# GpSimd's row sends behind marks of their point, the spectrum's negation a step sooner, and batch 0's rows stored by halves

## The chip, the cores and the metric

One core of one Trainium2 chip runs the whole program. The metric is the device time of one execution in microseconds (us). Three runs of the kernel before gave 1586.66 to 1594.67 us, median 1590.22.

## What is computed

For 8 batches of 2496 x 256 numbers: a Fourier transform along the sequence, a complex 256 x 256 mix of each frequency with a soft threshold, and the inverse transform. The 19968 rows of the result then go through a mixture of 8 experts, of which each row takes the best one.

```python
X = np.fft.rfft(x, axis=1)
Xr, Xi = (X.real.astype(np.float32), X.imag.astype(np.float32))
Yr = Xr @ w_r - Xi @ w_i + b_r
Yi = Xr @ w_i + Xi @ w_r + b_i
Yr = np.sign(Yr) * np.maximum(np.abs(Yr) - lam, 0.0)     # Yi alike
y = np.fft.irfft(Yr + 1j * Yi, n=x.shape[1], axis=1)
...
logits = x @ w_gate + modality_bias[modality_id]         # x: rows of y
e_idx = np.argmax(logits, axis=1)
...
h = np.maximum(x[mask] @ w1[e], 0.0)
out[mask] = gate_w[mask, None] * (h @ w2[e])
```

## The kernel before

The transform over 2496 = 39 x 64 points is done in matrix products. **Stage 1** (`s1_split`, `s1_chunk`) transforms over 39 points, in 11 chunks a batch: each chunk is split into a high and a low part (on GpSimd, L251, for chunks 0 to 5 of batches 2 and up), three products are summed, ScalarE copies them into a buffer `ev` (L275), and every two chunks SP stores the buffer to a scratch in DRAM, `scr` (L279). There are three such buffers. For batch 0 this is the program's start.

**The pairs**, ten points p a batch: `a_load` reads two of the 20 frequencies back from the scratch (L287), `s2_pair` transforms them (L296) and splits the result into `Xh` (ScalarE, L301, and the negated copy of the imaginary part, L303) and `Xl` (VectorE, L302 and L304); `mix_sums` has 24 products with the mixing matrix (L333); `shrink` is the soft threshold, on ScalarE (L341, `u`) and VectorE (L342, `s`); `is2_pair` transforms back over 64 (L357) into a buffer `z`. The loop is skewed: at point i it does the load of i+4, `s2` of i+2, the mix of i+1 and the inverse of i.

**The inverse over 39**, 22 pivots j a batch: `pivot` turns three columns of `z` with two products (L373, four instructions in a row) and splits them on ScalarE (L378, `ph`) and VectorE (L379, `pl`); `is1`, two pivots behind, has three products (L385 to L387) and a copy (L388). The stage 1 chunks 2 to 10 of batch b+2 stand between the pivots of b, so batches 6 and 7 have none.

**The route** of a batch (`Route.route`) runs beside the pairs of the next one: it finds each row's expert and its place, and at the end puts 22 sends on a list, `pending`. A send (`Route.scatter`, L541) is an indirect DMA from GpSimd that writes 117 rows of 264 numbers to their places in DRAM. GpSimd also splits the experts' weights (`SplitWeights.step`, L982 and L983), whose stores (L984, L985) SP issues. Four engines (TensorE, ScalarE, VectorE, GpSimd) run in the order in which the program is written; SP's loads and stores are held in place by `issue_after`. The sends are called at points 6 to 9, four at each, and one more ahead of each pivot, until the list is empty:

```python
                    if p > 5:
                        rt.scatter(4)
...
                for j in range(J):
                    rt.scatter(1)
                    pend.append((j, at.pivot(b, j)))
```

A send waits for its rows and its places alone, and for the landing of the eighth send before it.

**The experts** follow in 78 tiles of 256 rows: SP loads rows (L769) and weights (L751), two products per expert layer (L808, L838), and GpSimd sends the results (L851). The rows of the last batch are sent while the first tiles run.

## Time and profile before

| | |
|---|---|
| median of three runs | 1590.22 us |
| the profiled execution's own time | 1600.25 us |
| its span, first to last instruction | 1598.5 us |
| mean granted TensorE clock (share of full speed) | 0.975 |
| busy: TensorE, VectorE, ScalarE, GpSimd | 95%, 43%, 39%, 39% |
| first product of the experts (L808) | 686.37 us after the start |
| sends of rows (L541) before 680 us | 154, of 1.0 us each |

The busy shares are means over the span. The stages differ: the start, up to some 50 us; then one batch per 76 to 79 us, the pairs in 43 and the inverse in 26 to 32; and the experts from 686 us on. A view of a stretch tells more than the mean.

### The profile page before, as it was taken

To read this page: it belongs to the slowest core of one execution; us is meant where nothing else is said; L and a number is where in the kernel's file an instruction comes from. 1 tells how busy PE (TensorE), PEld (TensorE's weight loads), DVE (VectorE), ACT (ScalarE), POOL (GpSimd) and SP (SyncE) were. 2 spreads that over 40 slices of the span, in tenths; PEclk is the share of its full clock that TensorE was granted. 3 is DMA by queue.
4 is the path that set the end of the run, shared out by engine and by line. 5 is a ranking of instruction groups with operands and counts; after the bars stand their busy time and mean duration, and the time that the engine had idled before them with its cause. 6 is when DMAs were issued, how large, how long until landed. Compare 5 with 4: busy or idle time off the path is not lost. (4 is left out here: it accounts for less than half of the span.)

```text
span 1598.5 us, 34701 instructions
## 1 busy us (share of the span) xinstructions
PE 1521.1 (95%) x12459; PEld 1484.9 (93%) x12459; DVE 689.7 (43%) x1435; ACT 625.2 (39%) x1281; POOL 625.1 (39%) x629
## 2 busy tenths in 40 slices
PE   5899999999999889699999999999999999999998
PEld 4799898989898889599999999999999999899998
DVE  4466555656565555254333333333333333233332
ACT  4365656565656344242232323232223223232232
POOL 0054747475657544423642222232223223222232
PEclk8899999999999989799999999999999999999999
DMA  8788686858686536622442522752225227735441
GB/s 275 208 257 265 189 244 206 267 170 263 182 257 193 183 115 223 180 80 50 92 128 53 156 42 53 249 163 44 46 49 158 45 41 262 236 60 163 142 134 44
DMA packets 289103, 246.68 MB, mean 154 GB/s; under 512 B 207168, under 2 KB 242388, under 8 KB 285217
## 3 DMA queue, kind: packets, MB, share of 16 engines
q1 hardware_dynamic: 269937, 202.85, 44.9%
q0 software_dynamic: 18992, 41.58, 7.7%
q8 instruction: 100, 1.64, 0.4%
q14 instruction: 74, 0.61, 0.1%
HBM read 434.30 MB, written 100.73 MB: 335 GB/s over the span
## 5 line engine op out<-in xcount | busy, mean ns | idle before, releaser
L838 PE MATMUL y<-w,hh 128*128 128x256 f32 x2496 | 436.5, 278 | 0.0
L808 PE MATMUL h<-xh,w 128*128 128x256 f32 x2496 | 403.9, 278 | 3.8 <-DMA w<-wsp 3.8
L838 PEld LDWEIGHTS y<-w,hh 128*128 128x128 f32 x2496 | 378.4, 188 | 0.7 <-ACT hh L810 0.2
L838 PE MATMUL y<-w,hl 128*128 128x256 f32 x1248 | 347.6, 279 | 0.5 <-DVE hl L811 0.4
L808 PEld LDWEIGHTS h<-xh,w 128*128 128x128 f32 x2496 | 340.0, 189 | 4.3 <-issue 3.5
L851 POOL DMA_INDIRECT out<-o,ix x161 | 158.8, 986 | 430.5 <-ACT o L830 393.0
L811 DVE SCALAR_TENSOR_TENSOR hl<-h,hh 128x512 fp32r<-128x512 f32 x312 | 209.5, 689 | 231.8 <-ACT hh L810 192.1
L808 PE MATMUL h<-xl,w 128*128 128x256 f32 x1248 | 245.4, 278 | 0.0
L810 ACT ACTIVATE hh<-h 128x512 fp32r<-128x512 f32 x312 | 178.4, 596 | 155.4 <-PE h L808 140.9
L838 PEld LDWEIGHTS y<-w,hl 128*128 128x128 f32 x1248 | 234.2, 188 | 1.7 <-DVE hl L811 1.3
L333 PE MATMUL mx<-wmix,Xh 128*128 128x256 f32 x1280 | 187.3, 289 | 5.5 <-issue 4.7
L808 PEld LDWEIGHTS h<-xl,w 128*128 128x128 f32 x1248 | 189.5, 189 | 0.0
L788 POOL TENSOR_TENSOR xl<-tr,xh 128x512 fp32r<-128x512 f32 x78 | 101.1, 1296 | 206.7 <-ACT xh L787 205.4
L828 DVE TENSOR_SCALAR o<-y,xt 128x256 f32<-128x256 f32 x78 | 37.7, 484 | 316.9 <-ACT o L830 312.6
L333 PEld LDWEIGHTS mx<-wmix,Xh 128*128 128x128 f32 x1280 | 166.8, 194 | 8.2 <-issue 6.7
L830 ACT ACTIVATE o<-y,xt 128x256 f32<-128x256 f32 x78 | 37.1, 475 | 345.5 <-PE y L838 345.5
L373 PE MATMUL pv<-pv,z 128*120 128x136 f32 x704 | 115.8, 291 | 4.6 <-ACT z L360 4.3
L379 DVE TENSOR_TENSOR pl<-pv,ph 120x264 fp32r<-120x264 f32 x176 | 75.4, 431 | 102.0 <-ACT ph L378 73.9
L373 PEld LDWEIGHTS pv<-pv,z 128*120 128x120 f32 x704 | 103.2, 193 | 12.6 <-ACT z L360 5.8
L342 DVE SCALAR_TENSOR_TENSOR s<-mx,u 128x512 f32<-128x512 f32 (+1 forms) x81 | 55.5, 685 | 125.5 <-ACT u L341 113.9
L333 PE MATMUL mx<-wmix,Xl 128*128 128x256 f32 x640 | 103.0, 284 | 1.8 <-issue 1.8
L983 POOL TENSOR_TENSOR wl<-wr,wh 128x512 fp32r<-128x512 f32 x64 | 82.6, 1291 | 49.2 <-DMA wsp<-wl 46.3
(184 smaller groups left out, 2059.2 us busy)
## 6 DMA issues: line engine op xcount, KB each, us to landing
w<-wsp SPq DMA_DIRECT2D x166, 2048.0 KB
a<-scr SPq DMA_DIRECT2D x160, 128.0 KB
xt<-xs SPq DMA_DIRECT2D x624, 32.0 KB
scr<-ev SPq DMA_DIRECT2D x40, 480.0 KB
x<-in_x SPq DMA_DIRECT2D x37, 512.0 KB
wr<-in_moe_w SPq DMA_DIRECT2D x64, 256.0 KB
wsp<-wh SPq DMA_DIRECT2D x64, 256.0 KB
wsp<-wl SPq DMA_DIRECT2D x64, 256.0 KB
```

The costliest lines, as they stand in the source:

```text
L333: self.nc.tensor.matmul(ps[i][:, i, :], t[:, 2 * i + c, o:o + 128], self.w[:, wi, c, lo, :], start=False, stop=n == len(ops) - 1, skip_gro ...
L342: nc.vector.scalar_tensor_tensor(s, ps, LAM, u, ALU.add, ALU.min)
L373: nc.tensor.matmul(ps[:PK, c * 128:c * 128 + D // 2 + E], self.z[:, o:o + 3, :, :].rearrange("p n k r -> p (n k r)"), self.pv[:, c, :], st ...
L379: nc.vector.tensor_sub(pl, ps[:PK, :GC], ph)
L788: nc.gpsimd.tensor_sub(xl, tr, xh)
L808: nc.tensor.matmul(ps[:, q, :], w1[:, lo, c, f * 128:(f + 1) * 128], x[:, c, :], start=n == 0, stop=n == 5)
L810: nc.scalar.activation(hh[:, 2 * p:2 * p + 2, :], ps, AF.Relu)
L811: nc.vector.scalar_tensor_tensor(hl[:, 2 * p:2 * p + 2, :], ps, 0.0, hh[:, 2 * p:2 * p + 2, :], ALU.max, ALU.subtract)
L828: nc.vector.tensor_scalar_mul(o[:, s, :], y[s], gate)
L838: nc.tensor.matmul(y[s], lhsT, w2[:, lo, f, :], start=n == 0, stop=n == 23)
L851: ins = self.nc.gpsimd.indirect_dma_start(out=self.out, out_offset=bass.IndirectOffsetOnAxis(ap=ix, axis=0), in_=o, in_offset=None, bounds ...
L983: nc.gpsimd.tensor_sub(lo, raw, hi)
```

## The change

Three edits. First, `scatter` takes a mark, an instruction for which the sends of that call must wait. At points 6 to 9 one send waits for the negation that `s2` has just issued, and a second one for the `shrink` of the mix: eight sends in the pairs instead of sixteen. The other fourteen stand behind the pivots, one for each step of `j * 14 // 22`, and each waits for the `pl` of its pivot; the last is behind the last pivot. Second, `s2_pair` issues ScalarE's negation ahead of VectorE's first subtraction. Third, batch 0's stores are cut in two: partitions 0 to 59 of each buffer when it is full, the loads of pairs 0 to 3 behind the last of these, and partitions 60 to 119 after the loads. The load of pair 3 and the second step of the mixing matrix (`next(mixing)`) move accordingly.

```diff
--- before.py
+++ after.py
@@ -161,7 +161,7 @@
         self.ps = pool("ps", 2, space=PSUM)
         self.dr = pool("dr", 2, space=DRAM)
         self.scr = [None] * nb
-        self.xt, self.xs = {}, {}
+        self.xt, self.xs, self.parts = {}, {}, []
 
     def consts_first(self):
 
@@ -275,8 +275,19 @@
         nc.scalar.copy(self.ev[:, 2 * h:2 * h + 2, :].rearrange("p j d -> p (j d)"), ps[:PK])
         if h == 1 or c == 10:
             n = min(4, J - 4 * u)
-            rows = self.scr[b].rearrange("k (g j) d -> (k g) j d", g=3)
-            self.stored = nc.sync.dma_start(rows[:, 4 * u:4 * u + n, :], self.ev[:, :n, :])
+            if b == 0:
+                self.parts.append((self.ev, u, n))
+                self.s1_store(self.ev, u, n, 0, 60)
+            else:
+                self.s1_store(self.ev, u, n, 0, PK, b)
+
+    def s1_store(self, ev, u, n, lo, hi, b=0):
+        rows = self.scr[b].rearrange("k (g j) d -> (k g) j d", g=3)
+        self.stored = self.nc.sync.dma_start(rows[lo:hi, 4 * u:4 * u + n, :], ev[lo:hi, :n, :])
+
+    def s1_rest(self, b):
+        for ev, u, n in self.parts:
+            self.s1_store(ev, u, n, 60, PK)
 
 
     def a_load(self, b, p):
@@ -299,8 +310,8 @@
         xh = self.w2.tile([128, 4, 192], F32R, tag="Xh", name=f"Xh_{b}_{p}")
         xl = self.w2.tile([128, 4, 192], F32R, tag="Xl", name=f"Xl_{b}_{p}")
         nc.scalar.copy(xh[:, :, 64:192], ps)
+        self.mark = nc.scalar.mul(xh[:, :, 0:64], ps[:, :, 64:128], -1.0)
         nc.vector.tensor_sub(xl[:, :, 64:192], ps, xh[:, :, 64:192])
-        nc.scalar.mul(xh[:, :, 0:64], ps[:, :, 64:128], -1.0)
         nc.vector.tensor_sub(xl[:, :, 0:64], xh[:, :, 128:192], ps[:, :, 64:128])
         return xh, xl
 
@@ -339,7 +350,7 @@
         u, s = tl(self.w1, "u"), tl(self.w2, "s")
         ps = ps[beg][:, beg:end]
         nc.scalar.activation(u, ps, AF.Relu, bias=self.nlam)
-        nc.vector.scalar_tensor_tensor(s, ps, LAM, u, ALU.add, ALU.min)
+        self.mark = nc.vector.scalar_tensor_tensor(s, ps, LAM, u, ALU.add, ALU.min)
         return s
 
     def is2_pair(self, b, p, parts):
@@ -376,7 +387,7 @@
         ph = self.w2.tile([PK, GC], F32R, tag="ph", name=f"ph_{b}_{j}")
         pl = self.w2.tile([PK, GC], F32R, tag="pl", name=f"pl_{b}_{j}")
         nc.scalar.copy(ph, ps[:PK, :GC])
-        nc.vector.tensor_sub(pl, ps[:PK, :GC], ph)
+        self.mark = nc.vector.tensor_sub(pl, ps[:PK, :GC], ph)
         return ph, pl
 
     def is1(self, b, j, ph, pl, copy):
@@ -536,11 +547,13 @@
         nc.gpsimd.tensor_scalar_add(x1[:, :, 129], self.tok[:, j0:j1], float(b * SEQ))
         self.pending += [(si, j - j0, x1[:, j - j0, :]) for j in range(j0, j1)]
 
-    def scatter(self, n):
+    def scatter(self, n, mark=None):
         for si, k, rows in self.pending[:n]:
             i = self.nc.gpsimd.indirect_dma_start(
                 out=self.xs, out_offset=bass.IndirectOffsetOnAxis(ap=si[:, k:k + 1], axis=0),
                 in_=rows, in_offset=None, bounds_check=E * REG - 1, oob_is_err=False)
+            if mark is not None:
+                self.order(i, mark)
             self.note(i)
         self.pending = self.pending[n:]
 
@@ -1050,14 +1063,18 @@
                 ins = load(0)
             with tc.issue_after(ins.ins):
                 ins = load(1)
-            next(mixing, None)
+            with tc.issue_after(ins.ins):
+                load(2)
+                ins = load(3)
             at.s1_split(1, 0)
             at.s1_split(1, 1)
-            for c in range(4):
-                with tc.issue_after(ins.ins):
+            with tc.issue_after(ins.ins):
+                at.s1_rest(0)
+                for c in range(4):
                     at.s1_chunk(1, c, 2 if c < 2 else 0)
+                    if c == 1:
+                        next(mixing, None)
             with tc.issue_after(ins.ins):
-                load(2)
                 at.table_load("q", 0)
                 ins = at.s1_load(1, 2)
             bias(0)
@@ -1066,9 +1083,6 @@
             s2(1)
             at.s1_split(1, 4)
             mix(0)
-            with tc.issue_after(ins.ins):
-                ins = load(3)
-
             state = None
             routing = iter(())
             for b in range(nb):
@@ -1111,7 +1125,7 @@
                     if p < 6 if b > 0 else p > 4:
                         sw.step()
                     if p > 5:
-                        rt.scatter(4)
+                        rt.scatter(1, at.mark)
                     if p < 9:
                         bias(i + 2)
                     ending = i == last - 2
@@ -1119,6 +1133,8 @@
                         mix_last(i + 1, 0)
                     else:
                         mix(i + 1, 0 if apart else None)
+                    if p > 5:
+                        rt.scatter(1, at.mark)
                     if due:
                         state = next(routing, None)
                     at.is2_pair(b, p, ss.pop(i))
@@ -1143,8 +1159,9 @@
                     at.s1_chunk(*s1.pop(0), 0)
                 pend = []
                 for j in range(J):
-                    rt.scatter(1)
                     pend.append((j, at.pivot(b, j)))
+                    if j * 14 // 22 != (j - 1) * 14 // 22:
+                        rt.scatter(1, at.mark)
                     chunk = j % 2 == 1 and j != 15
                     if len(s1) > 4 and chunk:
                         at.s1_split(*s1[4])
@@ -1158,6 +1175,7 @@
                     next(routing, None)
                 for _ in routing:
                     pass
+                assert not rt.pending
                 bias(10 * b + 11)
                 ahead(10 * b + 10)
                 for jj, r in pend:
```

GpSimd's order in batch 1, from the split of chunk 1 of the batch after next at point 5 to the first pivots (`xs` are the rows in DRAM, `x1b` the results of the inverse, `si` the places, `x1l` the low part of a stage 1 chunk, `wh` a weight split). Before, where rows that repeat are folded into a count:

```order
L251 TENSOR_TENSOR x1l_1_1840<-x_0_1517,x1h_1_1839 117x512
L541 DMA xs<-x1b,si_0_1710 162048x264 x4
L251 TENSOR_TENSOR x1l_2_1906<-x_1_1586,x1h_2_1905 117x512
L541 DMA xs<-x1b,si_0_1710 162048x264 x4
L251 TENSOR_TENSOR x1l_3_1974<-x_1_1586,x1h_3_1973 117x512
L541 DMA xs<-x1b,si_0_1710 162048x264 x4
L251 TENSOR_TENSOR x1l_4_2049<-x_2_1651,x1h_4_2048 117x512
L541 DMA xs<-x1b,si_0_1710 162048x264 x4
L251 TENSOR_TENSOR x1l_5_2115<-x_2_1651,x1h_5_2114 117x512
L541 DMA xs<-x1b,si_0_1710 162048x264 x6
L982 CAST wh_6_2287<-wr_6_1734 128x512
```

And now, with what each waits for:

```order
L251 TENSOR_TENSOR x1l_1_1846<-x_0_1523,x1h_1_1845 117x512 [waits PE_49,Activation_49]
L552 DMA xs<-x1b,si_0_1716 162048x264 [waits DVE_49,Activation_49]
L552 DMA xs<-x1b,si_0_1716 162048x264 [waits DVE_49]
L251 TENSOR_TENSOR x1l_2_1906<-x_1_1592,x1h_2_1905 117x512 [waits PE_49,Activation_49]
L552 DMA xs<-x1b,si_0_1716 162048x264 [waits Activation_49]
L552 DMA xs<-x1b,si_0_1716 162048x264 [waits DVE_49]
L251 TENSOR_TENSOR x1l_4_2037<-x_2_1657,x1h_4_2036 117x512 [waits PE_49,Activation_49]
L552 DMA xs<-x1b,si_0_1716 162048x264 [waits Activation_49]
L552 DMA xs<-x1b,si_0_1716 162048x264 [waits DVE_49]
L251 TENSOR_TENSOR x1l_5_2097<-x_2_1657,x1h_5_2096 117x512 [waits PE_49,Activation_49]
L552 DMA xs<-x1b,si_0_1716 162048x264 [waits DMASW0_49,DVE_49]
L552 DMA xs<-x1b,si_0_1716 162048x264 [waits DMASW1_49,DVE_49]
```

Two sends instead of four stand between two subtractions, each behind ScalarE or VectorE, and the rest follow behind VectorE (the last two rows here are the first two of the fourteen), with a split of weights after six and one after twelve. The waits on DMASW are those for the eighth send before.

ScalarE and VectorE at the first pair (`s_0_0` is the transform in PSUM), before:

```order
L301 CAST Xh_0_308<-s_0_0_303 128x4x128 [waits PE_49]
L303 ACTIVATE Xh_0_308<-s_0_0_303 128x4x64 [waits DVE_49]
L301 CAST Xh_1_319<-s_0_1_314 128x4x128 [waits PE_49]
L302 TENSOR_TENSOR Xl_0_309<-s_0_0_303,Xh_0_308 128x4x128 [waits Activation_49]
L304 TENSOR_TENSOR Xl_0_309<-Xh_0_308,s_0_0_303 128x4x64 [waits Activation_49]
```

Now:

```order
L312 CAST Xh_0_317<-s_0_0_312 128x4x128 [waits PE_49]
L313 ACTIVATE Xh_0_317<-s_0_0_312 128x4x64
L312 CAST Xh_1_328<-s_0_1_323 128x4x128 [waits PE_49]
L314 TENSOR_TENSOR Xl_0_318<-s_0_0_312,Xh_0_317 128x4x128 [waits PE_49,Activation_49]
L315 TENSOR_TENSOR Xl_0_318<-Xh_0_317,s_0_0_312 128x4x64
```

ScalarE's negation waits for nothing but its place in the queue, and VectorE's second subtraction has lost its wait.

SP's order at the start, from batch 0's last store on (`scr_139` is batch 0's scratch, `scr_261` and `scr_269` batch 1's, `a_n` the load of pair n). Before:

```order
L279 DMA scr_139<-ev_5_236 120x512
L287 DMA a_0_243<-scr_139 64x2x256 x2
L287 DMA a_1_246<-scr_139 64x2x256 x2
L279 DMA scr_261<-ev_0_262 120x1024
L279 DMA scr_261<-ev_1_282 120x1024
L287 DMA a_2_294<-scr_139 64x2x256 x2
L186 DMA c_q<-in_c_q 128x512
L239 DMA x_66<-in_x 128x1024
L287 DMA a_3_357<-scr_139 64x2x256 x2
L186 DMA c_m<-in_c_m 128x512
```

And now, without the load of pair 1, and of the six stores of the second halves the first and the last:

```order
L286 DMA scr_139<-ev_5_236 60x512
L298 DMA a_0_243<-scr_139 64x2x256 x2
L298 DMA a_2_249<-scr_139 64x2x256 x2
L298 DMA a_3_252<-scr_139 64x2x256 x2
L286 DMA scr_139<-ev_0_140 60x1024
L286 DMA scr_139<-ev_5_236 60x512
L186 DMA c_q<-in_c_q 128x512
L286 DMA scr_269<-ev_0_270 120x1024
L186 DMA c_m<-in_c_m 128x512
L286 DMA scr_269<-ev_1_294 120x1024
L298 DMA a_4_368<-scr_139 64x2x256 x2
```

The loads of pairs 2 and 3 stand ahead of batch 1's stores and of the tables, and six more stores stand behind them, ahead of the first table.

## Rows read from the trace of the kernel before

**Rows 1.** The page, part 1: busy time, share of the span and instructions of each engine.

```profile
PE 1521.1 (95%) x12459; PEld 1484.9 (93%) x12459; DVE 689.7 (43%) x1435; ACT 625.2 (39%) x1281; POOL 625.1 (39%) x629
```

**Rows 2.** Busy time by stretch: the stretch and its length, then the busy time of TensorE (PE), its weight loads (PEld), VectorE, ScalarE and GpSimd (POOL) with their instructions, the granted TensorE clock, the DMA share and GB/s. The first five hold the last points of the pairs and the first half of the inverse of batches 1 to 5, the sixth is in the experts.

```profile
160.00:200.00 40.00, 36.38 (x279) 33.76 (x278) 21.17 (x44) 24.12 (x55) 31.69 (x32) 1.00 0.65 190
240.00:280.00 40.00, 37.67 (x284) 35.10 (x284) 22.07 (x48) 24.57 (x59) 31.60 (x32) 1.00 0.68 206
320.00:360.00 40.00, 36.38 (x257) 33.47 (x256) 21.12 (x45) 24.15 (x58) 28.37 (x29) 0.96 0.59 173
400.00:440.00 40.00, 37.39 (x267) 34.81 (x267) 21.37 (x48) 24.55 (x60) 26.49 (x28) 0.96 0.63 183
480.00:520.00 40.00, 37.40 (x284) 34.87 (x283) 21.16 (x48) 25.98 (x62) 28.25 (x32) 1.00 0.65 192
800.00:1000.00 200.00, 200.00 (x1732) 199.13 (x1732) 70.49 (x131) 61.46 (x112) 65.60 (x61) 1.00 0.36 86
```

**Rows 3.** The same view with the inverses of batches 0, 1, 6 and 7 as stretches, from the first product of the first pivot to the last product of the last.

```profile
105.20:131.02 25.82, 25.82 (x192) 24.33 (x191) 16.94 (x38) 19.91 (x50) 13.28 (x13) 1.00 0.86 268
177.81:208.19 30.38, 26.83 (x191) 24.43 (x192) 16.73 (x37) 20.47 (x51) 19.79 (x21) 1.00 0.67 194
571.29:599.81 28.52, 23.30 (x166) 21.91 (x165) 15.03 (x50) 12.73 (x35) 17.12 (x18) 0.88 0.40 134
655.12:686.54 31.42, 24.52 (x156) 23.53 (x157) 10.22 (x24) 14.79 (x44) 11.35 (x12) 0.78 0.41 120
```

**Rows 4.** GpSimd's timeline: start and duration in us, engine, line, operation, output and inputs, count, and in brackets the idle time before it and what ended it. Batch 1's first four sends, then the first and the last of twelve in batch 6's pairs, the first and the eighth in its inverse, the first and last of twelve and of ten in batch 7.

```profile
160.52 1.20 POOL L541 DMA_INDIRECT xs<-x1b,si  x1 [0.21 <-DVE Xl L302]
...
164.62 0.99 POOL L541 DMA_INDIRECT xs<-x1b,si  x1 [0.30 <-issue]
165.64 1.29 POOL L251 TENSOR_TENSOR x1l<-x,x1h 117x512 fp32r<-117x512 f32 x1
...
540.48 1.08 POOL L541 DMA_INDIRECT xs<-x,si  x1 [2.17 <-DVE x L535]
...
554.80 0.99 POOL L541 DMA_INDIRECT xs<-x,si  x1 [0.30 <-issue]
...
570.86 1.02 POOL L541 DMA_INDIRECT xs<-x,si  x1 [0.23 <-issue]
...
579.97 1.00 POOL L541 DMA_INDIRECT xs<-x,si  x1 [0.30 <-issue]
...
628.96 1.09 POOL L541 DMA_INDIRECT xs<-x1b,si  x1 [0.19 <-issue]
...
643.34 0.99 POOL L541 DMA_INDIRECT xs<-x1b,si  x1 [0.31 <-issue]
...
655.42 1.03 POOL L541 DMA_INDIRECT xs<-x1b,si  x1 [0.24 <-issue]
...
667.16 1.00 POOL L541 DMA_INDIRECT xs<-x1b,si  x1 [0.31 <-issue]
```

**Rows 5.** ScalarE's timeline, same columns: the rectifier of the soft threshold around the runs of twelve sends in batches 6 and 7.

```profile
537.37 0.69 ACT L341 ACTIVATE u<-mx,nlam 128x512 f32<-128x512 f32 x1
...
541.98 0.69 ACT L341 ACTIVATE u<-mx,nlam 128x512 f32<-128x512 f32 x1 [0.37 <-issue]
...
555.78 0.69 ACT L341 ACTIVATE u<-mx,nlam 128x512 f32<-128x512 f32 x1 [9.51 <-remote]
...
566.05 0.69 ACT L341 ACTIVATE u<-mx,nlam 128x512 f32<-128x512 f32 x1 [0.68 <-PE mx L333]
...
630.83 0.69 ACT L341 ACTIVATE u<-mx,nlam 128x512 f32<-128x512 f32 x1 [0.57 <-ACT mx L313]
...
646.32 0.69 ACT L341 ACTIVATE u<-mx,nlam 128x512 f32<-128x512 f32 x1 [9.07 <-remote]
```

**Rows 6.** TensorE's timeline, same columns: products of the inverse in batch 6 behind its eight sends, in batch 7 behind its ten, and two pivots, ten apart, after the sends have ended.

```profile
579.44 0.35 PE L385 MATMUL i<-ph,c_g 120*117 120x264 f32 x1 [2.27 <-issue]
...
582.82 0.57 PE L385 MATMUL i<-ph,c_g 120*117 120x264 f32 x1 [2.21 <-ACT x1b L388]
...
667.70 0.57 PE L385 MATMUL i<-ph,c_g 120*117 120x264 f32 x1 [4.97 <-ACT x L388]
...
675.99 0.63 PE L373 MATMUL pv<-pv,z 128*120 128x136 f32 x4
...
684.29 0.63 PE L373 MATMUL pv<-pv,z 128*120 128x136 f32 x4
```

**Rows 7.** SP's queue: start of the issue, duration until the last of the group is issued, line, operation, count. The first loads of pairs from batch 0's scratch, the first weights of the experts, and the weights that follow the last send of batch 6's rows.

```profile
26.73 2.59 SPq L287 DMA_DIRECT2D a<-scr  x4
...
631.02 0.94 SPq L751 DMA_DIRECT2D w<-wsp  x2
...
671.29 27.02 SPq L751 DMA_DIRECT2D w<-wsp  x4
```

**Rows 8.** Groups by line in the first 680 us: line, engine, operation, shape and count, then busy time and mean ns of one, then the idle time of the engine just before them and what ended most of it.

```profile
L303 ACT ACTIVATE Xh<-s 128x256 fp32r<-128x256 f32 x80 | 30.8, 385 | 91.6 <-DVE Xl L302 78.3 <-DVE omid L450 6.3 <-issue 6.3
```

**Rows 9.** TensorE's timeline at the start, columns as in rows 6: the first two pairs' transform, the third pair's, and a stage 1 chunk of batch 1.

```profile
30.37 3.78 PE L296 MATMUL s<-c_m,a 128*128 128x128 f32 x16 [5.57 <-DMA a<-scr]
...
41.95 2.05 PE L296 MATMUL s<-c_m,a 128*128 128x128 f32 x8 [4.83 <-issue]
...
74.88 0.59 PE L270 MATMUL s<-x1h,c_f 117*120 117x512 f32 x1 [2.79 <-DVE x1h L250]
```

## The prediction

> **What bounds the kernel now.** I read the page first: TensorE is busy for 95% of the span [rows 1]. Then the busy time by stage, because an average hides where the other 5% lies. In the expert phase nothing can be won: TensorE is busy for all 200 us between 800 and 1000 [rows 2]. The idle time is in the first 690 us, and in the windows that hold the last points of the pairs and the inverse of each batch. In those of batches 1 to 5 TensorE is idle for 3.62, 2.33, 3.62, 2.61 and 2.60 us of 40 [rows 2]. The inverse of batch 0 has no rows to send and no idle time in its 25.82 us; that of batch 1 takes 30.38 us with 26.83 busy, of batch 6 28.52 with 23.30, of batch 7 31.42 with 24.52 and a granted clock of 0.78 [rows 3]. So I looked at what GpSimd does there.
>
> GpSimd's timeline shows the sends back to back, one per 1.30 us, of which 1.00 is busy. In batch 1 they come by fours, with a subtraction of 1.3 us between the fours (160.52 to 164.62, then L251). In batches 6 and 7, which have no such subtraction, twelve come in one piece: 540.48 to 554.80 and 628.96 to 643.34. Then ten more follow in the inverse: the first eight at 570.86 to 579.97 in batch 6, all ten at 655.42 to 667.16 in batch 7 [rows 4]. Against these, ScalarE's timeline: the rectifier L341 runs every 4.6 us (537.37, 541.98), then not until 555.78, 9.51 us idle, "remote"; and again 9.07 us before 646.32 [rows 5]. Both ends lie 0 to 2 us behind the last send of a run. TensorE has the same in the inverse: 2.27 and 2.21 us idle at 579.44 and 582.82, 4.97 at 667.70 just behind the send of 667.16, while at 675.99 to 684.29, with no send, ten pivots take 8.30 us, 0.83 each [rows 6]. In each piece the first four to six sends cost nothing visible. My reading: while GpSimd issues sends without a gap, instructions and signals of the other engines arrive late; they live off what is already queued, and stop when that is used up.
>
> **The change, part by part.** Durations are of the profiled execution, 1600.25 us, which lies 10 us (0.6%) above the median of the runs, 1590.22. I take the sum off the median, since the terms are stalls of some us that are small against either.
>
> *The runs of twelve in the pairs.* What they cost is the time between rectifiers beyond 4.6 us [rows 5]: 541.98 to 555.78 is 13.8, so 9.2; the next two steps to 566.05 are 10.27 instead of 9.2, so 1.1 of half clock; 630.83 to 646.32 is 15.49, so 10.9. Together 21.2 us. After, points 6 to 9 hold two sends each, one behind ScalarE's negation and one behind VectorE's shrink of its own point: two per 4.6 us with 2.3 us on average from one to the next, less dense than the fours of batch 1, which passed. In the marked sends the wait also regulates itself, since a late engine holds the next send back. Bounds: 0 (the stall isn't the sends') to 21.2. I take **19.5**; the rest is the 2048 KB loads issued at 631.02 [rows 7], which share the stretch with batch 7's run.
>
> *Batches 1 to 5.* The idle times of the five windows add up to 14.8 us [rows 2], and 0.96 of the clock in two of them is 1.6 us each, 18.0 in all. What waits there is mostly the inverse, with ten sends. After, it holds fourteen, one per 1.57 pivots. With chunks of batch b+2 between them a pivot takes 25.82 / 22 = 1.17 us [rows 3], so a send comes every 1.84 us instead of 1.30, and 0.84 us of it is free instead of 0.30. Two splits of the experts' weights stand between GpSimd's sends there; their stores are wanted much later. Bounds: 4 x 5 more sends at today's 18.0 / 50 = 0.36 us, a loss of 7.2, to a gain of 18.0. I take **8**, since four fifths of the sends keep close company still.
>
> *The inverses of 6 and 7.* With 0.83 us a pivot and some 1.7 us to start and end, 20 us would do [rows 6]; batch 7 takes 31.42, and loses 11.4. Batch 6 loses 5.2 of idle time and 2.1 by half clock from 582.82 to 587 (4.2 us at half speed), 7.3. Together 18.7, or 0.94 us a send. Here the pace is 1.57 x 0.83 = 1.30 us a send, just that of a run without gaps, so the marks will hold sends back but leave little free time: fourteen alone need 18.2 us of GpSimd. Bounds: eight more sends at 0.94, a loss of 7.5, to a gain of 18.7. I take **10**, the middle of the part above zero.
>
> *Negation sooner.* It now follows the first copy on ScalarE at once. That engine stood idle for 78.3 us in 80 negations waiting for VectorE's L302, 0.98 us each [rows 8]. The first three products of a half need Xh, so a late Xh would be 0.9 us nearer; but the pairs are bound by TensorE's own sums, and only a pair that comes late uses it. Bounds -1 to +3; I take **0.5**.
>
> *Batch 0's stores by halves.* The first load from the scratch was issued at 26.73; TensorE waited 5.57 us for it until 30.37, then 4.83 us until 41.95, then 2.79 at 74.88 [rows 7, 9]. Now the loads of pairs 0 to 3 follow six stores of half the rows, and should be issued some 4 us sooner. Behind them stand six more stores on SP's queue, and batch 1's first copy into a store buffer waits until the second half has left it, which delays the sums ahead of the first pair by 2 to 3 us. Pair 2 no longer waits for a load. Bounds: a loss of 3 (the first pair late, nothing won behind) to a gain of 7 (5.57 + 4.83 less what the tables still need); I take **3**. The Trainium skill, "DMA: Bandwidth & Descriptors", in its table of patterns, says of two transfers to halves of the partitions not to bother, as they share the same engines and serialize. By it the first half lands at half time only because the other half is queued behind the loads, and the term is between 0 and 3; no run here shows it yet.
>
> *Behind the last batch.* The load at 671.29 is ordered behind the last send [rows 7]. That send moves from the fifth pivot to the last one, and the stage in front of the experts gets some 20 us shorter, while the loads need as long as before. Bounds 0 to 6 us of waiting; I take **-2**.
>
> Sum: 19.5 + 8 + 10 + 0.5 + 3 - 2 = 39 us, so 1590.2 - 39 = **1551 us**.
>
> **The rivals.**
> A, full cure: no stall is left, 21.2 + 18.0 + 18.7 + 3.5 - 2 = 59 us, 1531. For it: the marks regulate themselves, and the first sends of a run are free. Against it: the pace in batches 6 and 7.
> B, the stall is counted by sends in the inverse, at today's mean, (18.0 + 18.7) / 70 = 0.52 us: 98 sends take 51 of the 36.7 that they take now, so 14 of the 19.5 are given back, and 1584 is left.
> C, the other side: in the inverse no send is free, since a pivot is a chain over TensorE, ScalarE and VectorE with two steps in hand, and a send per 1.57 pivots hits each of them. At the 0.94 us of batches 6 and 7 the 98 sends cost 92 us against 36.7; with 21 won elsewhere (19.5 + 3.5 - 2), 34 us slower, 1624. It decides from (36.7 + 21) / 98 = 0.59 us a send. For it: 0.94 was measured. Against it: in these two batches the stall came behind the fourth or fifth send of a piece, and batches 1 to 5 show 0.36.
> D, late transfers: the experts' first rows and weights wait for the sends at the end of batch 7 and the shorter stage, 15 to 20 us of the gain come back as idle time of TensorE around the first tiles: 1570. For it: the order behind the last send. Against it: two loads of weights are issued ahead of it.
> E, it isn't the sends: the stalls coincide with them but come from the loads, and stay; 1590 - 3.5 + 2, some 1588. Against it: batch 6's run has no large load beside it, and stalls as long. The Trainium skill, "SBUF — State Buffer", on its two sides, holds that TensorE, ScalarE and VectorE's own port never wait on anyone and that a transfer and an engine's work can't slow each other; by this alone a gap between sends would bring nothing, which is rival E. The 9.51 us of ScalarE speak against it.
>
> **Chances.** Forecast 0.50 (1538 to 1568), A 0.17, B 0.10, C 0.08, D 0.10, E 0.05. A measurement tells some 0.5%, 8 us, from no change: faster is under 1582, slower over 1598. Faster takes the forecast, A, D and half of B, 0.82; the same is the other half of B and E, 0.10; slower is C, 0.08. The range, 1528 to 1582, takes in A, the forecast's bounds and D, and leaves B's upper half, C and E out, somewhat under 2 in 10.
>
> **What will show it.** Right: no two sends of a piece 1.30 us apart in the pairs; no gap over 2 us before L341's successor in batches 6 and 7; the two inverses at 23 to 26 us; batches 1 to 5 with under 2 us idle in their windows; the first pair's sums near 30 to 34 us and no wait of 4.83 behind them. Wrong: an inverse longer than before (C), gaps in the same places with spaced sends (E), or the first product of the experts waiting for a transfer for over 5 us (D).

## The result, and the profile after

The changed kernel takes 1551.86 us (median of four runs, 1548.6 to 1553.75), the kernel before 1590.93 in the same comparison: a ratio of 0.9753, 95% interval 0.9723 to 0.9783, 39 us faster. The profiled execution took 1551.3 us with a span of 1549.5.

Busy time by stretch, columns as in [rows 2, 3]; the five windows of batches 1 to 5, then the inverses of batches 1, 6 and 7:

```profile
160.00:200.00 40.00, 40.00 (x315) 38.37 (x314) 24.06 (x50) 26.73 (x62) 29.80 (x29) 1.00 0.66 192
240.00:280.00 40.00, 39.90 (x307) 37.93 (x307) 23.81 (x50) 27.98 (x66) 32.48 (x33) 1.00 0.79 232
320.00:360.00 40.00, 39.83 (x307) 37.86 (x306) 25.45 (x54) 26.87 (x66) 28.14 (x29) 1.00 0.76 227
400.00:440.00 40.00, 40.00 (x322) 38.66 (x321) 24.42 (x55) 25.62 (x62) 24.50 (x25) 1.00 0.85 262
480.00:520.00 40.00, 38.68 (x318) 37.38 (x317) 24.25 (x52) 21.35 (x50) 22.04 (x27) 1.00 0.72 220
...
179.02:204.80 25.78, 25.78 (x192) 24.29 (x191) 16.74 (x37) 19.92 (x51) 20.02 (x20) 1.00 0.77 224
542.01:566.94 24.93, 21.41 (x166) 19.97 (x165) 14.89 (x49) 12.84 (x36) 20.20 (x21) 1.00 0.45 145
610.72:637.90 27.18, 20.39 (x155) 18.97 (x156) 10.12 (x24) 14.59 (x44) 16.49 (x18) 0.99 0.65 158
```

Where 2.3 to 3.6 us were idle [rows 2], now at most 0.2 are, in batch 5's window 1.3. The inverse of batch 1, with fourteen sends in it, is as long as that of batch 0 with none. In the inverses of batches 6 and 7 the granted clock is back at 0.99 and above, and 3.5 and 6.8 us of idle time are left.

GpSimd's timeline, columns as in [rows 4], a piece of the inverses of batches 1, 6 and 7:

```profile
188.31 1.34 POOL L552 DMA_INDIRECT xs<-x1b,si  x1 [0.85 <-DVE pl L390]
...
196.07 0.99 POOL L552 DMA_INDIRECT xs<-x1b,si  x1 [0.30 <-issue]
198.12 0.99 POOL L552 DMA_INDIRECT xs<-x1b,si  x1 [1.06 <-DVE pl L390]
...
546.02 0.99 POOL L552 DMA_INDIRECT xs<-x,si  x1 [0.30 <-issue]
547.01 0.64 POOL L995 CAST wh<-wr 128x512 fp32r<-128x512 f32 x1
547.73 1.26 POOL L996 TENSOR_TENSOR wl<-wr,wh 128x512 fp32r<-128x512 f32 x1
549.18 1.01 POOL L552 DMA_INDIRECT xs<-x,si  x1 [0.19 <-DVE t_gba L703]
...
616.37 0.99 POOL L552 DMA_INDIRECT xs<-x1b,si  x1 [0.45 <-issue]
619.27 0.99 POOL L552 DMA_INDIRECT xs<-x1b,si  x1 [1.91 <-DVE pl L390]
```

In batches 1 and 7 the waits open gaps, here of 0.85 to 1.91 us, after three to five sends. In batch 6's inverse no wait does; there a split of the experts' weights (L995 and L996, some 2 us) stands behind every three or four sends. ScalarE's rectifier, columns as in [rows 5], in batch 6:

```profile
527.53 0.69 ACT L352 ACTIVATE u<-mx,nlam 128x512 f32<-128x512 f32 x1 [1.43 <-PE mx L344]
532.46 0.69 ACT L352 ACTIVATE u<-mx,nlam 128x512 f32<-128x512 f32 x1 [1.71 <-PE mx L344]
537.10 0.69 ACT L352 ACTIVATE u<-mx,nlam 128x512 f32<-128x512 f32 x1 [1.83 <-PE mx L344]
```

It keeps its step of 4.6 to 4.9 us, and what it waits for is TensorE. At the start things went the other way. ScalarE and TensorE, columns as in [rows 9]:

```profile
31.33 1.07 ACT L275 COPY ev<-s 120x512 f32<-120x512 f32 x2 [13.62 <-DMA scr<-ev]
```

```profile
31.97 0.78 PE L270 MATMUL s<-x1h,c_f 117*120 117x512 f32 x1 [12.63 <-ACT ev L275]
...
34.68 2.97 PE L307 MATMUL s<-c_m,a 128*128 128x128 f32 x16
...
42.74 1.22 PE L307 MATMUL s<-c_m,a 128*128 128x128 f32 x8 [2.25 <-issue]
...
75.16 0.75 PE L270 MATMUL s<-x1h,c_f 117*120 117x512 f32 x1 [3.69 <-DVE x1h L250]
```

The first pair's transform begins at 34.68 instead of 30.37, the third's at 42.74 instead of 41.95 [rows 9].

### The profile page after: what moved, and what is told of

It reads as the page before. It is cut to its first block, busy times and chain, and to the rows that moved or that the text cites. A ratio compares the mean times of both kernels' runs of the same rounds, so it can differ in the third digit from the quotient of the medians.

```text
span 1549.5 us, 34918 instructions
## 1 busy us (share of the span) xinstructions
PE 1499.1 (97%) x12459; PEld 1469.3 (95%) x12459; DVE 685.2 (44%) x1435; ACT 620.2 (40%) x1281; POOL 625.6 (40%) x629
## 5 line engine op out<-in xcount | busy, mean ns | idle before, releaser
L344 PE MATMUL mx<-wmix,Xh 128*128 128x256 f32 x1280 | 184.0, 287 | 0.0
L384 PE MATMUL pv<-pv,z 128*120 128x136 f32 x704 | 109.1, 279 | 1.8 <-DVE pl L390 1.3
L552 POOL DMA_INDIRECT xs<-x1b,si x88 | 90.6, 1030 | 42.8 <-DVE pl L390 14.8
L352 ACT ACTIVATE u<-mx,nlam 128x512 f32<-128x512 f32 (+1 forms) x81 | 55.2, 682 | 127.5 <-PE mx L344 112.8
L384 PEld LDWEIGHTS pv<-pv,z 128*120 128x120 f32 x704 | 97.3, 182 | 8.6 <-DVE pl L390 1.8
```

The lines of the kernel that those rows point to most:

```text
L344: self.nc.tensor.matmul(ps[i][:, i, :], t[:, 2 * i + c, o:o + 128], self.w[:, wi, c, lo, :], start=False, stop=n == len(ops) - 1, skip_gro ...
L352: nc.scalar.activation(u, ps, AF.Relu, bias=self.nlam)
L384: nc.tensor.matmul(ps[:PK, c * 128:c * 128 + D // 2 + E], self.z[:, o:o + 3, :, :].rearrange("p n k r -> p (n k r)"), self.pv[:, c, :], st ...
L552: i = self.nc.gpsimd.indirect_dma_start(out=self.xs, out_offset=bass.IndirectOffsetOnAxis(ap=si[:, k:k + 1], axis=0), in_=rows, in_offset= ...
```

## The experiments

Stage times below run from the first product of a batch's L357 (L368 after the change) to its first pivot ("pairs") and on to its last inverse product ("inverse"). By this count the pairs of the kernel before take 44.1 to 46.6 us in batches 1 to 5, and 52.9 and 52.5 in batches 6 and 7. Three chips were met. On the first (e1 to e4, and again e12) and the second (e5 to e8) the kernel before took 1593 and 1597 us; on the third it took 1551, and there twelve sends in one run held nothing up. That is why the three experiments on it (e9 to e11) have to be read apart, and why e12 was made. In the views, "remote" marks a wait whose end the trace ties to no instruction.

**e1, the waits taken out,** at all three calls. Places and numbers of sends stay.

```diff
-                        rt.scatter(1, at.mark)
+                        rt.scatter(1)
```

> The changed kernel with the same places of the sends in the program (eight in the pairs, fourteen in the inverse) but without their waits; batches 6 and 7 then send 22 rows in one run, 1.30 us apart, broken only by the route's three sums and the weights' splits. Theory 'gaps' (the other engines stall when sends come 1.3 us apart for more than four to six): the stalls come back in batches 6 and 7, 15 to 25 us, and part of those of batches 1 to 5; 1575 to 1600 us, a rectifier gap of over 5 us in both batches. Theory 'places' (fewer sends in the pairs are what helps, the waits do nothing): 1552 us, no such gap.

1576.1 us, ratio 0.9898 (0.9862 to 0.9934): between the two theories. The pairs of batches 6 and 7 take 43.2 and 43.7 us, near the changed kernel's 42.6 and 41.0, since six sends, not twelve, stand between the rows' readiness and the route's sums, on which GpSimd waits anyway; the rectifier's gap over 5 us that theory 'gaps' expected in both batches was 4.62 us in batch 6 and missing in batch 7. Batch 6's inverse, where weight splits break the sends, takes 24.5 us (24.9 with the waits). But the inverses of batches 1 to 5 take 28.0 to 31.2 us (144.6 together, 131.5 with the waits), and batch 7's 37.9, with sixteen sends in one run. TensorE there:

```profile
639.57 0.57 PE L396 MATMUL i<-ph,c_g 120*117 120x264 f32 x1 [5.82 <-issue]
...
648.73 0.57 PE L396 MATMUL i<-ph,c_g 120*117 120x264 f32 x1 [7.24 <-ACT x L399]
```

So of the 49 us between the profiled executions, 24 come with the new places (and the other two edits) and 25 with the waits. The medians on this chip, 1593.5 before, 1576.1 without waits and 1548.7 with them (e2), say 17 and 27.

**e2, the first edit alone** in the kernel before (marks and places as in the change, the rest untouched).

```diff
-                        rt.scatter(4)
+                        rt.scatter(1, at.mark)
...
+                    if p > 5:
+                        rt.scatter(1, at.mark)
...
-                    rt.scatter(1)
                     pend.append((j, at.pivot(b, j)))
+                    if j * 14 // 22 != (j - 1) * 14 // 22:
+                        rt.scatter(1, at.mark)
```

> The kernel before with the first edit alone (marks and places of the sends; negation and stores as before). If the sends are all of it: 1547 to 1553 us, since the stores by halves made the changed kernel's start 1.4 us longer by its trace, with first sums of batch 1's pairs at 133.7 us instead of 135.1, and the negation is worth under 1 us. If negation or stores had a share of the gain: 1555 to 1565 us.

1548.7 us, ratio 0.973 (0.9691 to 0.9769). Within the noise the sends are all of the gain.

**e3, waits, but four sends behind each.**

```diff
-                    if p > 5:
-                        rt.scatter(1, at.mark)
...
-                        rt.scatter(1, at.mark)
+                        rt.scatter(4, at.mark)
...
-                    if j * 14 // 22 != (j - 1) * 14 // 22:
-                        rt.scatter(1, at.mark)
+                    if j == 0:
+                        rt.scatter(6, at.mark)
```

The call behind the negation is gone; the four stand behind the shrink.

> The changed kernel with waits kept but four sends behind each shrink of points 6 to 9 and six behind the first pivot: the numbers of before, each group behind a mark. Four sends take 5.2 us, a point 4.6, so in batches 6 and 7 they run together again. Theory 'gaps': the stalls of batches 6 and 7 come back, each over 5 us in front of a rectifier or in the inverse, 1570 to 1592 us. Theory 'marks' (what helps is that a send never starts before its point's result): within 4 us of the changed kernel, 1548 to 1556.

1606.66 us, ratio 1.0084 (1.0055 to 1.0114), slower than before and than either theory said. The stalls of batches 6 and 7 came back in part, smaller than the 5 us expected (a rectifier gap of 3.31 us in batch 6, idle times of 3.44 and 3.76 in batch 7's inverse). What neither theory had counted: the inverses of batches 1 to 5 take 34 us, because the sends start later, and the subtractions of stage 1, queued behind four of them, come late. TensorE in batch 1:

```profile
192.72 0.49 PE L272 MATMUL s<-x1l,c_f 117*120 117x512 f32 x1 [4.01 <-POOL x1l L251]
```

In these five inverses TensorE waits 21.0 us for L251, so the 1607 us are late subtractions more than stalls. What e3 shows of the stall lies in batches 6 and 7: behind marks too, runs of eight to ten sends held the others up, in the pairs less than before (47.2 and 41.7 us against 52.9 and 52.5).

**e4, gaps without waits** in batches 6 and 7 of the kernel before.

```diff
             self.note(i)
+            if gap:
+                self.gaps()
...
+    def gaps(self):
+        for _ in range(2):
+            self.nc.gpsimd.memset(self.idle, 0.0)
...
-                        rt.scatter(4)
+                        rt.scatter(4, b > 5)
...
-                    rt.scatter(1)
+                    rt.scatter(1, b > 5)
```

> The kernel before, without any mark, in batches 6 and 7 alone two small GpSimd memsets behind each send, some 0.5 us, so a send every 1.8 us instead of 1.3; places and numbers as before. Theory 'gaps': the rectifier gaps of 9.51 and 9.07 us shrink below 3 us and these two batches win most of the 29 us that the change won in them; by the times, where the profile's stalls are some 10 us longer than those of a run without one, 1565 to 1575 us. Theory 'marks': gaps as before, since no send waits for a result; 1588 to 1594.

1583.57 us, ratio 0.9935 (0.9916 to 0.9953): the stalls went, but only 10 us of the time, where 15 to 25 were expected. A send came every 2.1 us, not 1.8 as expected. Pairs and inverse of batch 6, then of batch 7:

```profile
518.48:561.43 42.95, 42.79 (x377) 42.56 (x376) 28.39 (x65) 19.64 (x38) 24.15 (x41) 1.00 0.59 188
561.43:583.43 22.00, 21.26 (x166) 19.99 (x165) 15.10 (x50) 12.72 (x35) 15.80 (x33) 1.00 0.19 58
586.24:638.27 52.03, 40.96 (x337) 40.39 (x335) 23.89 (x51) 17.89 (x35) 29.08 (x44) 0.90 0.70 240
638.27:661.17 22.90, 21.00 (x156) 20.33 (x157) 10.19 (x24) 14.68 (x44) 17.30 (x34) 0.93 0.63 146
```

The inverses are shorter than in the changed kernel, and no rectifier waits for "remote". But GpSimd, now late, held up two others, as TensorE shows:

```profile
609.70 0.31 PE L509 MATMUL rk<-oh,tri 117*117 117x184 bf16 x1 [9.37 <-POOL oh L496]
...
683.05 0.77 PE L815 MATMUL h<-xh,w 128*128 128x256 f32 x2 [7.72 <-DMA w<-wsp]
```

The first is a memset of the route behind GpSimd's queue; the second the experts' weights, which are ordered behind the last send.

**e5, e6, e8: the stores by halves.** One set on one chip; e8 is the changed kernel, e5 has the third edit undone (the lines with a minus of its part of the change stand again), e6 has the second halves ahead of the loads of pairs 2 and 3:

```diff
             with tc.issue_after(ins.ins):
+                at.s1_rest(0)
                 load(2)
                 ins = load(3)
...
             with tc.issue_after(ins.ins):
-                at.s1_rest(0)
                 for c in range(4):
```

> The changed kernel with the third edit undone: batch 0's rows are stored whole, loads and tables in the order of before; marks and the sooner negation stay. If the halves cost what the changed kernel's trace shows (end of batch 0's pairs 1.4 us later): 1 to 3 us faster than the changed kernel of this set, 1546 to 1552 us, inverse of batch 0 from 105.0 us or sooner. If the halves win 3 us, as was forecast: 3 us slower than it. Against the kernel with the marks alone it tells the sooner negation: theory 'pairs are bound by TensorE', within 1 us in the end of batch 0's pairs and no change of the pairs of batches 1 to 5, 43.9 us.

> The changed kernel with the six stores of the second halves ahead of the loads of pairs 2 and 3 instead of behind them. Theory 'late second half' (ScalarE's first copy of batch 1 stands still until the first buffer's second half has left, and everything behind it on TensorE): that copy starts 2 to 3 us sooner than 31.33, first transform of a pair at 32 instead of 34.68, end of batch 0's pairs 1 to 3 us sooner; 1548 to 1551. Rival 'pair 2 then waits for its load': its sums start where they started before, 42.7, and nothing is won.

> The changed kernel itself, for comparison within this set: 1549 to 1553 us.

e8 took 1554.9 us (ratio 0.9744, 0.9718 to 0.977), e5 1555.1 (0.9729, 0.9701 to 0.9756), e6 1558.7 (0.9767, 0.9743 to 0.979): by time the halves can't be told from none, and all three lie above the ranges expected. By the traces batch 0's pairs end at 105.0 us in e8 and at 102.6 and 103.6 in e5 and e7, which store whole buffers, so the halves cost 1.4 to 2.4 us at the start on this chip, and later differences cover it (in e5's profiled execution, the slowest of its five, batches 1 to 5 take 6.5 us longer than in e8). In e6 the first copy did start sooner, at 28.93 instead of 31.45, but pair 2 then waited for its load until 44.65 (e8: 42.99), as the rival said, and the first L368 came at 51.0 instead of 47.4. The negation can't be told apart by time: e5 has it, e2 hasn't, their ratios are 0.9729 and 0.973, and both have pairs of 43.9 us in batches 1 to 5. But batch 0's pairs end at 102.6 us in e5 and at 105.4 in e2, where within 1 us was expected. Part of this is a wait of TensorE for a cast on VectorE, before and after the change:

```profile
64.16 0.46 PE L270 MATMUL s<-x1h,c_f 117*120 117x512 f32 x1 [2.01 <-DVE x1h L250]
```

```profile
63.59 0.46 PE L270 MATMUL s<-x1h,c_f 117*120 117x512 f32 x1 [1.75 <-DVE x1h L250]
```

It is 2.00 or 2.01 us in all four traces without the sooner negation and 1.74 or 1.75 in all ten with it, whatever the chip: VectorE's second subtraction (L304), just ahead of the cast, has lost its wait of 0.45 us. A second such wait (74.88 in [rows 9]) falls from 2.8 to 3.8 us to 1.75 in e5 and e7; as these ran on another chip than e2, e4 and e12, that share isn't certain.

**e7, twelve and ten in batches 6 and 7,** each with one memset behind it, on e5:

```diff
-                        rt.scatter(1, at.mark)
+                        rt.scatter(1 + (b > 5), at.mark, b > 5)
...
-                    if j * 14 // 22 != (j - 1) * 14 // 22:
-                        rt.scatter(1, at.mark)
+                    left = 10 if b > 5 else 14
+                    if j * left // 22 != (j - 1) * left // 22:
+                        rt.scatter(1, at.mark, b > 5)
```

> Marks and sooner negation, whole stores, and in batches 6 and 7 twelve sends in the pairs and ten in the inverse, each followed by one GpSimd memset of 0.25 us, so that sends stand some 1.65 us apart at the closest. Theory 'gaps': the inverses of these batches go down from 24.9 and 27.2 us towards the 22.0 and 22.9 us that 2.1 us between sends gave, 3 to 6 us won over the whole stores alone: 1543 to 1549. Rival 'GpSimd's time' (the later sends hold up what follows on GpSimd, as the 2.1 us did in front of the route's memset and of the experts' second weights): the same or slower than the whole stores alone, with a wait for GpSimd in the pairs of batch 7 or for the weights at the first tiles.

1553.58 us, ratio 0.9739 (0.9712 to 0.9766): nothing won over e5. The inverses fell to 23.4 and 24.7 us (e5: 25.6 and 26.5), but the pairs rose to 43.8 and 45.1 (42.6 and 41.7). In batch 7's pairs nine sends stood 1.4 to 1.5 us apart (1.65 was expected), and TensorE waited 3.77 us near the end of them. So 1.45 us a send was still too close in a run of nine, where 2.1 us in e4 was not.

**e9 to e11: the cost by itself,** at point 2 of batch 3 of the changed kernel, where no send stands.

```diff
+                    if b == 3 and p == 2:
+                        rt.extra()      # e9: 12 sends again; e10: 48 memsets; e11: 12 plain dma_start
```

> The changed kernel with twelve more sends in one run, at point 2 of batch 3, where no send stands otherwise: twelve rows of batch 1 once more to the same places. The suspected cost by itself. Theory 'gaps': a rectifier gap of 8 to 10 us behind the fourth to sixth send, pairs of batch 3 at 52 to 54 us instead of 43.9, batches 1, 2 and 4 as in the changed kernel; total 7 to 10 us more. Rival 'end of the pairs' (the stall needs what stands in the last points: the route's end, the expert loads, the store traffic): pairs of batch 3 within 1 us of 43.9.

> The changed kernel with 48 memsets of some 0.25 us on GpSimd at the same point, as long as twelve sends, without any transfer. Theory 'the send itself' (issuing an indirect transfer is what holds the others up): pairs of batch 3 at 43.9 us, no gap. Rival 'GpSimd busy without a pause': the same 8 to 10 us as twelve sends.

> The changed kernel with twelve plain transfers of the same rows from GpSimd to twelve pieces of a buffer in DRAM at the same point: the same bytes from the same queue, with no list of places. If what holds the others up is any transfer that GpSimd issues: a gap as with twelve sends, as far as they come as close. If it is the indirect form: pairs of batch 3 within 2 us of 43.9.

1547.9, 1547.39 and 1545.69 us; the kernel before took 1551.13 on that chip, so the ratios (0.9972, 0.9976, 0.9962) are not those of the other sets. All three have pairs of 43.9 us in batch 3, also behind twelve sends 1.30 us apart. Taken alone e9 would refute the theory; with the kernel before itself at 1551 on this chip, it says that this chip doesn't stall. The disturbances weren't free even so: the inverse of batch 3 takes 34.4, 31.2 and 32.5 us instead of 25.8, since GpSimd is late, and TensorE waits for the subtractions L251 (6.26, 3.27 and 3.80 us in all). e9's pairs and inverse of batch 3, and what the inverses of batches 6 and 7 take there, with fourteen sends in each:

```profile
277.99:321.87 43.88, 43.88 (x382) 43.58 (x380) 25.77 (x54) 22.88 (x46) 26.34 (x28) 1.00 0.72 229
321.87:356.26 34.39, 28.13 (x192) 25.57 (x191) 17.97 (x37) 20.43 (x51) 28.91 (x30) 0.95 0.75 217
546.18:568.74 22.56, 21.55 (x166) 20.01 (x165) 16.00 (x49) 12.99 (x36) 18.32 (x19) 1.00 0.45 149
613.42:634.42 21.00, 19.39 (x156) 18.72 (x157) 10.18 (x24) 14.70 (x44) 15.80 (x17) 1.00 0.73 192
```

**e12, all three in the kernel before,** one batch each: memsets in batch 2, sends in 3, plain transfers in 4.

```diff
+                    if p == 2:
+                        rt.extra(b)
```

> The kernel before with three disturbances at point 2 of the pairs: batch 2 has 48 GpSimd memsets (13 us), batch 3 twelve more sends in one run, batch 4 twelve plain transfers from GpSimd to a buffer of their own. Batches 6 and 7 stay as a control. In the set before this one the kernel before itself took 1551 us instead of 1593 and 1597, on another chip of the same kind, and its twelve sends held nothing up. Theory 'gaps, on such chips as stall': where this run's kernel before takes about 1590 us, a gap of 8 to 10 us in batch 3, none in batch 2, and in batch 4 between none and 5; where it takes about 1551, no gap in batch 3 nor in batches 6 and 7. Rival 'end of the pairs': gaps in 6 and 7 with none in batch 3. Rival 'GpSimd busy': a gap in batch 2 as well.

1636.61 us, ratio 1.0222 (1.0185 to 1.0259), on a chip where the kernel before took 1597.89. The pairs of batches 2, 3 and 4:

```profile
209.53:253.42 43.89, 43.89 (x382) 43.59 (x381) 27.61 (x54) 23.34 (x46) 30.48 (x70) 1.00 0.71 220
294.77:349.22 54.45, 49.02 (x382) 46.90 (x380) 27.45 (x54) 22.68 (x45) 33.02 (x35) 0.91 0.67 208
389.49:433.69 44.20, 44.05 (x381) 43.40 (x379) 26.61 (x54) 22.72 (x45) 27.43 (x35) 1.00 0.79 255
```

GpSimd and ScalarE in batch 3:

```profile
304.08 1.03 POOL L543 DMA_INDIRECT xs<-x,si  x1 [0.19 <-issue]
...
318.36 0.99 POOL L543 DMA_INDIRECT xs<-x,si  x1 [0.30 <-issue]
```

```profile
315.66 0.69 ACT L341 ACTIVATE u<-mx,nlam 128x512 f32<-128x512 f32 x1 [6.63 <-remote]
...
321.42 0.59 ACT L301 CAST Xh<-s 128x512 fp32r<-128x512 f32 x1 [5.07 <-remote]
```

In the pairs that is 10.5 us for twelve sends, in the middle of them, with no expert load near; nothing for 13.5 us of unbroken memsets; 0.3 for as many rows sent plainly, which GpSimd issued in 7.8 us. The control batches 6 and 7 stalled as before (pairs of 51.4 and 50.8 us). That settles the cause of the stall, on this chip: a run of indirect sends, not GpSimd's busy time, not the number of bytes, not the place in the program. Whether it is the list of places or the scattered rows in DRAM that does it wasn't tried. The rest of the 39 us lies in the inverses of these three batches (38.7, 37.6 and 38.7 us against 27.0, 31.8 and 28.1), and is another cost: GpSimd is late after each of the three, the memsets too, and TensorE waits for its subtractions behind the sends, in batch 2 the longest:

```profile
265.41 0.78 PE L272 MATMUL s<-x1l,c_f 117*120 117x512 f32 x1 [5.37 <-POOL x1l L251]
```

## Why the prediction was right

The time came out at 1551.9 where 1551 was forecast. The mechanism of the forecast holds, but its terms don't all, and that the total came out to 1 us is luck: two errors stand against each other. By the profiled executions:

| term | forecast | measured | from |
|---|---|---|---|
| runs of twelve in the pairs of 6 and 7 | 19.5 | 21.8 | 52.9 to 42.6, 52.5 to 41.0 us |
| batches 1 to 5 | 8 | 20.4 | 384.7 to 364.3 us together |
| inverses of 6 and 7 | 10 | 7.8 | 28.5 to 24.9, 31.4 to 27.2 us |
| negation | 0.5 | 0.3 seen, within the next row | one wait of batch 0, 2.01 to 1.75 us |
| start | 3 | -1.4 | batch 1's first L357 from 133.7 to 135.1 us |
| in front of and in the experts | -2 | 0.3 | 912.1 to 911.8 us from the first tile on |
| sum | 39 | 48.9 | spans: 49.0 |

*The runs of twelve.* Right in cause and size. Of the 21.8 us, e1 keeps 18.5 without any wait (pairs of 43.2 and 43.7), so here the smaller number of sends in one piece did most, and not the spacing that the term was built on. With 42.6 and 41.0 us the pairs of 6 and 7 are free of it; the loads beside batch 7, for which I kept something back, cost nothing visible.

*Batches 1 to 5.* The step that failed is "since four fifths of the sends keep close company still". They do stand 1.30 us apart by threes, but the wait for `pl` opens a gap whenever the pivots are behind, and that is enough: the inverses lost 14.3 us, to within 2.5 of five times 25.8, and the pairs and the passage to the inverse 6.1. The gain is even 2.4 over my upper bound of 18.0. That bound counted idle time and half clock; idle time outside the windows is only some 0.2 us, but in these five stages TensorE's busy time fell too, from 356.4 to 349.4 us, of which the bound held 3.2. e1 shows that the waits did it in the inverses: without them the same places give back 13.1 us of the 14.3. The pairs' 6.1 came with the places, as e1 keeps them. Not all of the 14.3 is the stall: in batches 1, 3 and 5 of the kernel before, TensorE waited 1.21, 1.22 and 0.93 us for a subtraction L251 behind four sends, and doesn't now.

*Inverses of 6 and 7.* Right in kind and near in size. What is left against 22.6 and 21.0 us on the chip that doesn't stall is 2.4 and 6.2 us, and its longest waits stand behind runs of three to five sends. Batch 7's 27.2 us misses the 23 to 26 that were to show it.

*Start.* Wrong in sign, within its bounds. The load was issued 3.7 us sooner, at 23.02, as I had it (some 4). But the step "delays the sums ahead of the first pair by 2 to 3 us" was too small: the copy waited until 31.33, the transform came 4.3 us later, and pair 2 had nothing left to win. The Trainium skill's advice on halves ("DMA: Bandwidth & Descriptors", its table of patterns) agrees with the outcome of e5 and e8, where the halves cost 2.4 us of the start; what costs here is the copy that waits for the second half to leave its buffer (13.62 us idle).

*From the profiled execution to the median.* Batches 1 to 5 were sized 12 us short, and yet the total fits, because I took a sum read from one execution off the median. That execution, 1600.25 us, lies above all four runs of before in the comparison, and before's runs spread by 14 us on one chip (1585 to 1599 in the set of e1 to e4). The changed kernel's profiled execution lies at its median. So the 49 us between the traces are 39 between the medians. That the stalls were longer in that execution isn't shown: e4, the same program up to batch 6, takes 384.3 us for batches 1 to 5 in an execution at its median, against 384.7, and e2 on the same chip 363.6; the controls of e12 are 2.6 us shorter in batches 6 and 7 together. Where the rest of the 10 us lies stays open. Had I sized batches 1 to 5 rightly, I should have said 1539.

*The rivals.* C needed 0.59 us a send in the inverse; measured against 25.8 us for batches 1 to 5 and 22.0 and 21.0 for 6 and 7 (e4, e9), the 98 sends cost 2.5 + 2.9 + 6.2 = 11.6 us, 0.12 each. That sends clustered in the inverse can make the kernel slower than before e3 shows, but by late subtractions (21.0 us); a price like C's stands only in one long run (e1, batch 7: 37.9 us with sixteen sends). B is refuted by the same number, D by the experts' time, E by e12. A came nearest: some 9 us of stall are left in batches 6 and 7. The Trainium skill ("SBUF — State Buffer", on its two sides) would have priced the stalls at nothing; it speaks of ports, and whatever is held up here, the measurement decides: e12 shows ScalarE standing for 6.63 and 5.07 us beside sends and not beside plain transfers.

*The other signs.* In the pairs of batches 6 and 7 sends still come 1.30 us apart by twos and threes, where none were to, without a gap over 2 us before a rectifier. The first pair's transform, at 34.68 us, came just behind the 30 to 34, with 2.25 us of idle time behind it instead of 4.83. No wait for a transfer stands in front of the experts.

## What to carry to other kernels

Read idle "remote" time of an engine against what GpSimd issues at that moment: runs of eight to sixteen indirect transfers 1.3 us apart held up TensorE, ScalarE and VectorE on the first chip (e1, e3, e12), and breaking them up by places and by waits that open by themselves won 45 us there (e2). On the second chip the kernel before is as slow, though only nine sends 1.4 us apart were traced there (e7); on the third twelve in a run held nothing up. Before spacing transfers by fixed gaps, look at what is queued behind them: e4 cured the stall and lost 17 us (9.37 and 7.72) to late work on GpSimd. And what is summed from one execution belongs to that execution's time: here it lay 10 us above the median, and 49 us between two traces were 39 between the medians.

## What the runs showed of the hardware

One chip of three doesn't show the stall: the kernel before takes 1551.13 us there (25 runs) against 1593.46 and 1597.42, and twelve sends in a run cost nothing in the pairs where they stood. The first chip, met again in e12, stalled again. What the change is worth on the third was not measured by itself; with each of the disturbances of e9 to e11 in it, the changed kernel is 3 to 5 us faster than the kernel before. As these lengthen the inverses by 5 to 9 us, an estimate from their stage times is 1539 to 1541 us without them, 10 to 12 us faster. Why chips differ, and which resource a run of sends takes from the others, stays open. What the traces show is only its form: in e12, from the seventh send on until 2 us behind the last, TensorE goes on in pieces of one to four products, 0.2 to 1.0 us idle before each:

```profile
314.12 0.28 PE L333 MATMUL mx<-wmix,Xh 128*128 128x256 f32 x1 [0.80 <-issue]
...
317.70 0.37 PE L333 MATMUL mx<-wmix,Xh 128*128 128x256 f32 x1 [1.03 <-issue]
...
319.83 1.10 PE L333 MATMUL mx<-wmix,Xh 128*128 128x256 f32 x3 [1.03 <-issue]
```
